# An RWKV attention and a gated feed-forward layer: the sign word made by GpSimd, and a new written order

## The chip, the cores and the metric

The kernel runs on one core of one Trainium2 chip. The metric is the device time of one execution in microseconds (us), the median of three runs. A core has five engines that each work through their own queue in order: TensorE (PE, with the loads of its stationary operand shown as PEld), VectorE (DVE), ScalarE (ACT), GpSimd (POOL) and the sync engine (SP), which here issues all the DMAs.

## The reference

```python
def _attn_ref(r, k, v, w, u):            # B 4, H 8, S 768, D 48
    state = np.zeros((B, H, D, D)); y = np.zeros_like(r)
    for t in range(S):
        kt, vt, rt = (k[:, :, t], v[:, :, t], r[:, :, t])
        cur = np.einsum('bhd,bhe->bhde', u[None] * kt, vt)
        y[:, :, t] = np.einsum('bhd,bhde->bhe', rt, state + cur)
        state = w[None, :, :, None] * state + np.einsum('bhd,bhe->bhde', kt, vt)
    return y

def _moe_ref(x, w_gate, w_val, w_out):   # 3072 tokens, d_model 384, d_ff 1536
    gate = 1.0 / (1.0 + np.exp(-(x @ w_gate)))
    return gate * (x @ w_val) @ w_out
```

The output of the attention, as 3072 rows of 384, is the input `x` of the second function. The three weight matrices come to the chip as 64-bit floating-point numbers, and the kernel turns them into 32-bit numbers itself.

## The kernel before

The attention is done in 12 chunks of 64 tokens, each in two groups of heads, so there are 24 groups `n`. For a group: `L` and `X` load its channels (512 KB) and tokens (400 KB); `A`, `R`, `k`, `T` scale keys and queries by powers of `w`; `Z` makes the scores on PE; `K` masks them on VectorE; `I` applies them and the state on PE; `O` makes the state's increment on PE; `d` (ScalarE) and `s` (VectorE) bring the state on; `h` (ScalarE) and `l` (VectorE) write the output as a rounded part and a rest into the tile `xt`; `F` moves the 16 channels left over into their places with small DMAs.

Two chunks of all batches make a tile of 512 tokens, and there are six. Each tile goes through 12 weight blocks `f`: `U` is 18 matmuls of 512 columns into two PSUM banks of a ring of three, `g` a sigmoid on ScalarE, `m` a product on VectorE, `H` the rounded part of it on ScalarE, `q` its rest on GpSimd (`qv`: on VectorE), and `D` nine matmuls into three accumulators. Block 0 of the first tile is done in two halves of 256 columns, so that `U.0`, `U.1` are the halves, `U.2` is block 1 and `U.8` block 7.

A weight block is made ready once, while the first tile is worked on. `W` loads it (1152 KB for 128 x 1152 numbers of 64 bits; block 0 in two halves). `c` on ScalarE scales the high 32-bit word, read as a float, by 2^-112 into `wf`. `j` (`join_words`) on VectorE makes the 32-bit number: shift by three, put the sign of the high word in, put the three top bits of the low word in. `w` on ScalarE rounds it into the first half of `wx`, and `o` on GpSimd (`ov`: on VectorE) writes the rest into the second half. `wx` lies in the place of the raw words `wr`.

The order of the first 13 items, from the first load to the start of the second tile, is written out as a list of steps, `START`; behind the dot stands the group, the block or the item. Each engine gets its instructions in this order. Behind the list a loop runs over the remaining items of the other five tiles with its own fixed order.

A step that waits holds back every later step of its engine: this goes for SP's queue of DMAs as for the others.

Of the kernel before, what the change touches and what calls it, by code (L numbers as in the profile page):

```python
# [39 lines left out]


START = """
tc L.0 L.1 X.0 X.1 W.0 tk L.2 X.2 A.0 ti.1 Rv.0 A.1 k.0 ti.0 Z.0 Rv.1 k.1 tp L.3 c0.1 c0.0 K.0 tt
tn T.0 j0.1 I.0 T.1 Z.1 h.0 A.2 R.2 O.0 l.0 w0.1 K.1 T.2 F.0 X.3 W.1 o0.1 W.2 s.0 W.3 L.4 j0.0 I.1
O.1 h.1 k.2 X.4 s.1 w0.0 Z.2 l.1 A.3 o0.0 L.5 K.2 c.1 F.1 U.0 k.3 Rv.3 c.2 Tv.3 Z.3 j.1 g.0 I.2
m.0 w.1 K.3 O.2 R.4 H.0 X.5 h.2 qv.0 W.4 ov.1 d.2 W.5 L.6 l.2 c.3 s.2 F.2 j.2 I.3 A.4 O.3 R.5 h.3
X.6 d.3 W.6 l.3 W.7 W.8 w.2 s.3 F.3 j.3 U.1 A.5 D.0 g.1 U.2 m.1 w.3 ov.2 H.1 ov.3 c.4 qv.1 c.5 k.4
Tv.4 Z.4 g.2 k.5 Tv.5 D.1 L.7 m.2 K.4 H.2 U.3 q.2 j.4 Z.5 g.3 m.3 w.4 I.4 K.5 H.3 O.4 h.4 R.6 ov.4
D.2 X.7 d.4 W.9 W.10 q.3 W.11 A.6 l.4 s.4 F.4 c.6 j.5 I.5 O.5 h.5 R.7 d.5 A.7 l.5 s.5 F.5 w.5 k.6
U.4 Tv.6 j.6 Z.6 g.4 ov.5 w.6 D.3 m.4 c.7 o.6 K.6 H.4 U.5 j.7 c.8 g.5 qv.4 w.7 j.8 I.6 O.6 h.6 D.4  # L50
d.6 m.5 w.8 l.6 s.6 F.6 H.5 ov.7 U.6 qv.5 c.9 ov.8 k.7 c.10 Tv.7 j.9 Z.7 g.6 D.5 m.6 U.7 w.9 K.7
H.6 o.9 j.10 g.7 q.6 c.11 I.7 O.7 h.7 D.6 d.7 m.7 l.7 H.7 s.7 F.7 w.10 q.7 j.11 U.8 ov.10 D.7 w.11
g.8 ov.11 U.9 m.8 H.8 q.8 D.8 g.9 m.9 H.9 L.8 X.8 U.10 q.9 D.9 g.10 m.10 H.10 U.11 q.10 A.8 R.8
k.8 T.8 D.10 g.11 m.11 H.11 U.12 q.11 D.11 g.12 m.12 H.12 qv.12
"""


# [1 line left out]
def rwkv_then_moe(ctx: ExitStack, tc: tile.TileContext, wd, ch, tk, wt, rk0, vn0, wd0, out):  # L59
    nc = tc.nc  # L60
# [151 lines left out]
    def scale_words(f, c):  # L212
        if f not in w32:
            w32[f] = wtmp.tile([P, W3], F32, name="wf")
        words = raw[f].bitcast(F32).rearrange("q (n two) -> q n two", two=2)
        nc.scalar.activation(w32[f][:, c], words[:, c, 1], AF.Copy, scale=2.0**-112)  # L216

    def join_words(f, c):
        words = raw[f].bitcast(I32).rearrange("q (n two) -> q n two", two=2)
        low, high = words[:, c, 0], words[:, c, 1]  # L220
        g = w32[f].bitcast(I32)[:, c]
        nc.vector.tensor_scalar(g, g, 3, None, ALU.logical_shift_left)
        nc.vector.scalar_tensor_tensor(g, high, -(2**31), g, ALU.bitwise_and, ALU.bitwise_or)
        nc.vector.scalar_tensor_tensor(g, low, 29, g, ALU.logical_shift_right, ALU.bitwise_or)

    def round_weights(f, c):
        if f not in wparts:
            wparts[f] = wp.tile([P, 2, W3], F32R, name="wx", tag=f"w{f}")
            whi[f], wlo[f] = wparts[f][:, 0], wparts[f][:, 1]
        nc.scalar.copy(out=whi[f][:, c], in_=w32[f][:, c])  # L230
# [256 lines left out]
    def accumulators():  # L487
        return [pacc.tile([P, 512], F32, name=f"acc{d}") for d in range(3)]
# [298 lines left out]
```

## Time and profile before

| | |
|---|---|
| median of three runs | 580.67 us (579.79 to 582.91) |
| the profiled execution | 580.07 us, its span 578.3 us |
| PE busy | 534.4 us, 92% of the span |
| VectorE, ScalarE, GpSimd busy | 211.7, 189.4 and 146.1 us |
| mean granted TensorE clock | 0.972 |

The profiled execution lies 0.6 us under the median and inside the runs' spread; 1.8 us of it are outside the span. PE is busy nearly all of the time from about 110 us on, so the head of the program, in which the written order rules, is where PE is idle.

### The profile page before, as it was taken

Reading aid. Unit: us, or ns where it says so; the run is one execution under the profiler, and the core shown is the slowest. Engines: PE = TensorE matmul, PEld = TensorE weight load, DVE = VectorE, ACT = ScalarE, POOL = GpSimd, SP = SyncE. Lnnn points to the kernel's source line nnn. Section 1 sums busy time; section 2 is a strip of 40 time slices with the busy share of each in tenths; the row PEclk is TensorE's granted clock in tenths of the full one; section 3 lists DMA queues with packets and bytes.
Section 4 is the critical chain, followed back from the end, with each engine's and each line's share of the span. In section 5 each row is a group of like instructions: output and inputs, shape, how many; then the busy total and the mean of one; then the engine's idle time right before and its main releaser. Section 6 shows DMA issues by size and latency. Waiting matters only on the chain. (4 is left out here: it accounts for less than half of the span.)

```text
span 578.3 us, 12857 instructions
## 1 busy us (share of the span) xinstructions
PE 534.4 (92%) x5689; PEld 431.4 (75%) x5689; DVE 211.7 (37%) x338; ACT 189.4 (33%) x420; POOL 146.1 (25%) x125
## 2 busy tenths in 40 slices
PE   3646987999999999999999999999999999999994
PEld 2635766788778878788888788888788788888883
DVE  7896899931422322412312313313313312200101
ACT  4365465432422322322322323323413212212211
POOL 3420320323232222222322313313312211221220
PEclk9766999999999999999999999999999999999998
DMA  8498340130410113320113220013130001100001
GB/s 313 160 396 329 134 203 10 22 128 0 141 48 1 29 48 84 104 83 1 35 41 84 79 109 1 13 63 85 59 128 2 9 2 19 56 0 1 1 0 60
DMA packets 13261, 44.54 MB, mean 77 GB/s; under 512 B 2096, under 2 KB 2736, under 8 KB 11792
## 3 DMA queue, kind: packets, MB, share of 16 engines
q1 hardware_dynamic: 13200, 43.66, 21.8%
q8 instruction: 46, 0.75, 0.5%
q14 instruction: 15, 0.12, 0.1%
HBM read 36.58 MB, written 4.72 MB: 71 GB/s over the span
## 5 line engine op out<-in xcount | busy, mean ns | idle before, releaser
L443 PE MATMUL ring<-xt,wx 128*128 128x512 f32 (+1 forms) x1314 | 319.8, 396 | 14.2 <-DMA xt<-xt 7.6
L443 PEld LDWEIGHTS ring<-xt,wx 128*128 128x128 f32 x1314 | 245.4, 191 | 72.6 <-issue 9.7
L465 POOL TENSOR_TENSOR h<-sg,h 128x512 fp32r<-128x512 f32 x68 | 89.6, 1317 | 362.3 <-ACT h L461 362.3
L481 PE MATMUL acc<-h,wx 128*128 128x512 f32 (+1 forms) x657 | 163.7, 394 | 0.4 <-POOLq L613 0.4
L456 DVE TENSOR_TENSOR sg<-ring,sg 128x512 f32<-128x512 f32 (+1 forms) x73 | 49.9, 684 | 289.4 <-PE ring L443 289.4
L481 PEld LDWEIGHTS acc<-h,wx 128*128 128x128 f32 x657 | 121.2, 189 | 27.6 <-POOLq L613 0.8
L461 ACT CAST h<-sg 128x512 fp32r<-128x512 f32 (+1 forms) x73 | 44.8, 614 | 148.8 <-DVE sg L456 148.8
L452 ACT ACTIVATE sg<-ring 128x512 f32<-128x512 f32 (+1 forms) x73 | 43.2, 591 | 143.3 <-PE ring L443 143.2
L323 DVE COPY_PREDICATED score<-masks,sc 128x512 f32<-128x512 int32 x48 | 36.1, 753 | 14.8 <-PE sc L315 14.0
L265 POOL TENSOR_TENSOR dec<-chan,tabk 128x512 f32<-128x512 f32 x21 | 28.2, 1342 | 20.2 <-DVE wx L233 12.8
L259 ACT ACTIVATE dec<-chan,wu 128x128 f32<-128x128 f32 x96 | 30.7, 399 | 3.0 <-DMA chan<-in_ch 3.0
L402 ACT CAST xt<-ring 112x256 fp32r<-112x256 f32 (+1 forms) x52 | 17.1, 375 | 39.8 <-PE ring L284 39.8
L406 DVE TENSOR_TENSOR xt<-ring,xt 112x256 fp32r<-112x256 f32 (+1 forms) x52 | 19.9, 418 | 26.6 <-ACT xt L402 25.2
L315 PE MATMUL sc<-dec,chan 48*64 48x64 f32 x768 | 17.2, 231 | 9.8 <-DVE chan L271 7.3
L284 PEld LDWEIGHTS ring<-dec,state 48*48 48x48 f32 (+1 forms) x704 | 13.3, 130 | 14.0 <-issue 8.7
L369 ACT ACTIVATE state<-state,pw 112x96 f32<-112x96 f32 x80 | 23.5, 366 | 0.0
L315 PEld LDWEIGHTS sc<-dec,chan 48*64 48x64 f32 x768 | 14.8, 145 | 11.6 <-DVE chan L271 7.3
L284 PEld LDWEIGHTS ring<-score,toks 64*48 64x48 f32 (+1 forms) x768 | 14.5, 136 | 10.9 <-issue 6.6
L284 PE MATMUL ring<-dec,state 48*48 48x64 f32 (+1 forms) x704 | 16.7, 227 | 6.4 <-ACT sg L452 4.6
L284 PE MATMUL ring<-score,toks 64*48 64x64 f32 (+1 forms) x768 | 18.0, 234 | 3.8 <-DVE score L323 2.4
L216 ACT ACTIVATE wf<-wr 128x1152 f32<-128x1152 f32 (+1 forms) x13 | 15.3, 1189 | 15.7 <-DMA wr<-in_wt 10.1
L275 POOL TENSOR_TENSOR toks<-toks,tabn 128x384 f32<-128x384 f32 x17 | 18.0, 1059 | 8.8 <-ACT tabn L181 8.8
(52 smaller groups left out, 211.1 us busy)
## 6 DMA issues: line engine op xcount, KB each, us to landing
wr<-in_wt SPq DMA_DIRECT2D x11, 1152.0 KB, 9.0
chan<-in_ch SPq DMA_DIRECT2D x24, 512.0 KB, 4.9
toks<-in_tk SPq DMA_DIRECT2D x24, 400.0 KB, 5.1
out_y<-wf SPq DMA_DIRECT2D x17, 256.0 KB, 2.3
xt<-xt SPq DMA_DIRECT2D x30, 64.0 KB, 2.3
wr<-in_wt SPq DMA_DIRECT2D x2, 576.0 KB, 7.2
xt<-xt SPq DMA_DIRECT2D x12, 32.0 KB, 4.9
out_y<-sg SPq DMA_DIRECT2D x2, 128.0 KB, 3.2
```

What stands on the lines that cost most here:

```text
L259: nc.scalar.activation(t[:, 1, cs], k[:, cs], AF.Copy, scale=wu[:, 1, 4 * g + m : 4 * g + m + 1])
L265: eng.tensor_tensor(v4(t[:, 0]), v4(chan[n][:, 0]), bc2(table_of(n)[:, :, ::-1]), ALU.mult)
L284: nc.tensor.matmul(yb[n][bank][64 * half : 64 * half + m, cs], lhsT, rhs, start=first, stop=stop, skip_group_check=True,)
L315: nc.tensor.matmul(sc[64 * gm : 64 * gm + 64, be, o : o + C], kk[row, cs : cs + C], rr[row, cs : cs + C], start=True, stop=True,)
L323: nc.vector.copy_predicated(t.rearrange("q (b m i) -> q b m i", b=2, m=4), masks[:, m].bitcast(I32).unsqueeze(1).unsqueeze(1).broadcast_to ...
L369: nc.scalar.activation(st[:, p, s], st[:, p, s], AF.Copy, scale=pw[0:112, 4 * g + 2 * p + s, 64:65],)
L443: nc.tensor.matmul(o[:, self.cols], w[a][:, g * DM + kt * P : g * DM + (kt + 1) * P], self.x[:, kt, b, self.cols], start=(k == 0), stop=(k ...
L452: nc.scalar.activation(sg[:, c], self.pair[f][0][:, c], AF.Sigmoid)
L456: nc.vector.tensor_tensor(sg[:, c], self.pair.pop(f)[1][:, c], sg[:, c], ALU.mult)
L461: nc.scalar.copy(out=h[:, 0, c], in_=sg[:, c])
L465: eng.tensor_tensor(h[:, 1, c], self.sg.pop(f)[:, c], h[:, 0, c], ALU.subtract)
L481: nc.tensor.matmul(self.acc[d][:, self.cols], w[a][:, 2 * DM + d * P : 2 * DM + (d + 1) * P], h[:, b, self.cols], start=(f == 0 and k == 0 ...
```

## The change

The middle one of the three VectorE passes of `join_words` falls away. A new step `z` on GpSimd reads the high words as floats, compares them with zero, multiplies the 0 or 1 by -2^31 and writes the result as an integer over the high words. That is the sign bit, or zero. VectorE then shifts and joins this sign in one pass, and joins the low word in a second. `z` of a block must come behind `c` of the block, which reads the high words, and ahead of its `j`.

The list `START` is written anew. It holds a `z` for each block, and a new step `N` of nine matmuls of the identity with itself (128 x 128), whose result nobody reads. Of the steps that can run on either engine, `o` and `T` stand more often on GpSimd: ahead of `U.8` the list had `ov` seven times and has it five times, `Tv` five times and now twice, `qv` four times and now twice. The loads stand in another order, and `l.3` now stands ahead of `O.3`.

```diff
-tc L.0 L.1 X.0 X.1 W.0 tk L.2 X.2 A.0 ti.1 Rv.0 A.1 k.0 ti.0 Z.0 Rv.1 k.1 tp L.3 c0.1 c0.0 K.0 tt
...
+L.1 tk W.0 L.0 tc ti.0 A.1 tp tt R.1 c0.1 ti.1 k.1 X.0 X.1 N.9 Rv.0 W.1 z0.1 A.0 tn L.2 X.2 c0.0
...
+    def sign_words(f, c):
+        high = raw[f].bitcast(F32).rearrange("q (n two) -> q n two", two=2)[:, c, 1]
+        out = raw[f].bitcast(I32).rearrange("q (n two) -> q n two", two=2)[:, c, 1]
+        nc.gpsimd.tensor_scalar(out, high, 0.0, -(2.0**31), ALU.is_lt, ALU.mult)
+
     def join_words(f, c):
         words = raw[f].bitcast(I32).rearrange("q (n two) -> q n two", two=2)
-        low, high = words[:, c, 0], words[:, c, 1]
+        low, sign = words[:, c, 0], words[:, c, 1]
         g = w32[f].bitcast(I32)[:, c]
-        nc.vector.tensor_scalar(g, g, 3, None, ALU.logical_shift_left)
-        nc.vector.scalar_tensor_tensor(g, high, -(2**31), g, ALU.bitwise_and, ALU.bitwise_or)
+        nc.vector.scalar_tensor_tensor(g, g, 3, sign, ALU.logical_shift_left, ALU.bitwise_or)
         nc.vector.scalar_tensor_tensor(g, low, 29, g, ALU.logical_shift_right, ALU.bitwise_or)
...
+    def idle_matmuls(k):
+        t = pacc.tile([P, 512], F32, name="acc2")
+        for _ in range(k):
+            nc.tensor.matmul(t[:, 0:P], ident, ident, start=True, stop=True)
...
+        "N": idle_matmuls,
+        "z": lambda f: sign_words(f, ALL), "z0": lambda j: sign_words(0, HALVES[j]),
```

The queue of SP at the start, before (`chan` is filled by `L`, `toks` by `X`, `wr` by `W`, and `xt<-xt` are the small DMAs of `F.0`):

```order
L101 DMA chan<-in_ch 128x1024 x2
L106 DMA toks<-in_tk 128x800 x2
L210 DMA wr<-in_wt 128x576 x2
L101 DMA chan<-in_ch 128x1024
L106 DMA toks<-in_tk 128x800
L101 DMA chan<-in_ch 128x1024
L410 DMA xt<-xt 16x2x256 x6
L106 DMA toks<-in_tk 128x800
L210 DMA wr<-in_wt 128x1152 x3
```

And after:

```order
L102 DMA chan<-in_ch 128x1024
L211 DMA wr<-in_wt 128x576 x2
L102 DMA chan<-in_ch 128x1024
L107 DMA toks<-in_tk 128x800 x2
L211 DMA wr<-in_wt 128x1152
L102 DMA chan<-in_ch 128x1024
L107 DMA toks<-in_tk 128x800
L211 DMA wr<-in_wt 128x1152
L102 DMA chan<-in_ch 128x1024
L107 DMA toks<-in_tk 128x800
L211 DMA wr<-in_wt 128x1152
L416 DMA xt<-xt 16x2x256 x6
```

Block 0 is now loaded between the two first groups' channels, and three more blocks (1, 2 and 7) stand ahead of the small DMAs, where none stood before.

GpSimd from the rest of block 0 to the rest of the next block that it makes (`wx`), before (`dec` are the queries of `R`, `h` the rests of `q`):

```order
L233 TENSOR_TENSOR wx<-wf,wx 128x576 x2
L265 TENSOR_TENSOR dec<-chan,tabk 128x512 x2
L465 TENSOR_TENSOR h<-sg,h 128x512
L265 TENSOR_TENSOR dec<-chan,tabk 128x512
L465 TENSOR_TENSOR h<-sg,h 128x512
L265 TENSOR_TENSOR dec<-chan,tabk 128x512
L233 TENSOR_TENSOR wx<-wf,wx 128x1152 x2
```

And after, with the passes of `z` (`wr<-wr`) and a `T` (`toks`):

```order
L239 TENSOR_TENSOR wx<-wf,wx 128x576 x2
L271 TENSOR_TENSOR dec<-chan,tabk 128x512
L223 TENSOR_SCALAR wr<-wr 128x1152
L271 TENSOR_TENSOR dec<-chan,tabk 128x512
L223 TENSOR_SCALAR wr<-wr 128x1152
L281 TENSOR_TENSOR toks<-toks,tabn 128x384
L239 TENSOR_TENSOR wx<-wf,wx 128x1152
L471 TENSOR_TENSOR h<-sg,h 128x256
```

`z` of blocks 1 and 2 and the rest of block 1 (`o.1`) have come between, and GpSimd has more to do in the same stretch.

VectorE at the join of block 2 and the state of group 3, before:

```order
L222 TENSOR_SCALAR wf<-wf 128x1152
L223 SCALAR_TENSOR_TENSOR wf<-wr,wf 128x1152
L224 SCALAR_TENSOR_TENSOR wf<-wr,wf 128x1152
L406 TENSOR_TENSOR xt<-ring,xt 48x2x128 x4
L379 TENSOR_TENSOR state<-state,ring 112x2x96 x2
```

And after:

```order
L229 SCALAR_TENSOR_TENSOR wf<-wf,wr 128x1152
L230 SCALAR_TENSOR_TENSOR wf<-wr,wf 128x1152
L277 TENSOR_TENSOR chan<-chan,tabk 128x512
L412 TENSOR_TENSOR xt<-ring,xt 48x2x128 x4
L385 TENSOR_TENSOR state<-state,ring 112x2x96 x2
```

The join has two passes instead of three, and the keys of group 4 (`k.4`, `chan`) now stand between it and `l.3`, behind which `O.3` on PE now waits.

More of the change, by code (lines that the diff above doesn't have):

```diff
@@ L42 @@
 START = """
-tc L.0 L.1 X.0 X.1 W.0 tk L.2 X.2 A.0 ti.1 Rv.0 A.1 k.0 ti.0 Z.0 Rv.1 k.1 tp L.3 c0.1 c0.0 K.0 tt
[L44 to L54, printed above, removed]
+L.1 tk W.0 L.0 tc ti.0 A.1 tp tt R.1 c0.1 ti.1 k.1 X.0 X.1 N.9 Rv.0 W.1 z0.1 A.0 tn L.2 X.2 c0.0
+k.0 Z.0 j0.1 z0.0 K.0 T.0 T.2 c.1 I.0 h.0 T.1 O.0 j0.0 Z.1 W.2 L.3 s.0 w0.1 l.0 X.3 K.1 W.7 w0.0
+I.1 o0.1 A.2 O.1 Rv.2 h.1 F.0 o0.0 A.3 k.2 s.1 Z.2 l.1 R.3 U.0 K.2 c.2 k.3 L.4 g.0 I.2 h.2 O.2 z.1
+R.4 d.2 X.4 z.2 Z.3 A.4 j.1 W.5 m.0 L.5 W.3 T.3 H.0 l.2 K.3 s.2 j.2 I.3 w.1 o.1 h.3 k.4 W.11 q.0
+R.5 d.3 c.3 l.3 W.4 O.3 F.2 s.3 Z.4 w.2 W.6 U.1 z.3 Tv.4 A.5 g.1 ov.2 L.7 k.5 m.1 H.1 D.0 q.1 j.3
+K.4 U.2 c.4 g.2 m.2 w.3 D.1 U.3 H.2 L.6 z.4 ov.3 j.4 g.3 X.5 Z.5 I.4 O.4 W.8 c.5 K.5 m.3 W.10 q.2
+z.5 R.6 h.4 D.2 l.4 d.4 s.4 H.3 j.5 A.6 I.5 d.5 h.5 T.5 O.5 k.6 w.5 o.5 A.7 s.5 X.6 F.1 l.5 qv.3
+w.4 Z.6 U.4 g.4 Rv.7 c.7 D.3 ov.4 k.7 K.6 z.7 c.6 U.5 g.5 m.4 z.6 Z.7 H.4 I.6 d.6 Tv.6 O.6 j.7 j.6
+h.6 w.6 X.7 m.5 s.6 H.5 l.6 q.4 F.6 ov.6 D.4 K.7 c.8 U.6 q.5 w.7 g.6 W.9 ov.7 z.8 D.5 c.9 m.6 H.6
+j.8 q.6 U.7 g.7 I.7 T.7 F.5 O.7 D.6 F.4 z.9 w.8 d.7 o.8 h.7 m.7 H.7 s.7 l.7 c.10 qv.7 j.9 U.8 g.8
+z.10 D.7 m.8 w.9 H.8 o.9 c.11 qv.8 F.3 j.10 U.9 g.9 F.7 D.8 L.8 X.8 U.10 z.11 m.9 w.10 j.11 H.9
+g.10 qv.9 m.10 H.10 w.11 qv.10 A.8 R.8 k.8 T.8 o.10 D.9 U.11 ov.11 g.11 m.11 D.10 H.11 U.12 qv.11
+g.12 m.12 H.12 qv.12 D.11
 """
```

## The prediction

> **What bounds the kernel now.** I read the strips of the page first, then four windows, then PE in order of time, then the forms on VectorE and GpSimd. The strip shows PE at its limit from the eighth slice on, with gaps only ahead of it.
>
> ```profile
> PE   3646987999999999999999999999999999999994
> ...
> GB/s 313 160 396 329 134 203 10 22 128 0 141 48 1 29 48 84 104 83 1 35 41 84 79 109 1 13 63 85 59 128 2 9 2 19 56 0 1 1 0 60
> ```
>
> In the windows the columns are the length, then the busy time of PE, PEld, VectorE, ScalarE and GpSimd with their instructions, the granted clock, the DMA share and GB/s.
>
> ```profile
> 0.00:13.00 13.00, 3.21 (x73) 2.68 (x76) 9.64 (x22) 5.54 (x13) 3.63 (x15) 1.00 0.83 311
> 13.00:49.00 36.00, 17.66 (x530) 16.20 (x531) 31.08 (x48) 19.10 (x46) 11.27 (x8) 0.69 0.73 278
> 49.00:111.20 62.20, 56.03 (x830) 45.25 (x830) 55.82 (x66) 33.68 (x61) 13.36 (x7) 0.96 0.35 134
> 111.20:578.30 467.10, 457.50 (x4262) 367.28 (x4262) 115.17 (x204) 131.11 (x302) 117.87 (x95) 0.99 0.15 47
> ```
>
> Behind 111.2 us PE works 457.50 of 467.10 us: nothing in the change touches that work, and a start of `U.8` that comes earlier by some us ends the kernel earlier by as much. Ahead of it VectorE is the fullest engine: 86.9 of the 98.2 us between 13 and 111.2, and 55.82 of 62.20 in the later part, where PE has only 6.17 us to lose. GpSimd works 24.6 us in the two windows. PE in order of time gives the four places on which I build (start, duration, idle time ahead with its releaser):
>
> ```profile
> 8.23 1.08 PE L315 MATMUL sc<-chan,dec 48*64 48x64 f32 x32
> 11.37 1.09 PE L176 MATMUL acc<-ident,sg 128*128 128x128 f32 x4 [2.06 <-DVE sg L170]
> ...
> 49.00 4.18 PE L443 MATMUL ring<-xt,wx 128*128 128x256 f32 x18 [7.64 <-DMA xt<-xt]
> ...
> 111.17 4.44 PE L443 MATMUL ring<-xt,wx 128*128 128x512 f32 x18 [0.99 <-DVE sg L456]
> ```
>
> The first scores end at 9.31, `U.1` starts at 49.00 behind a wait of 7.64 us for the small DMAs of `F.2`, and `U.8` starts at 111.17.
>
> **What VectorE loses.** The forms (count, then busy us and mean ns):
>
> ```profile
> L223 DVE SCALAR_TENSOR_TENSOR wf<-wr,wf 128x1152 int32<-128x1152 int32 x11 | 17.0, 1548 | 0.4
> ...
> L224 DVE SCALAR_TENSOR_TENSOR wf<-wr,wf 128x1152 int32<-128x1152 int32 x11 | 15.9, 1444 | 0.4
> L233 DVE TENSOR_TENSOR wx<-wf,wx 128x1152 fp32r<-128x1152 f32 x9 | 12.4, 1385 | 0.0
> ...
> L222 DVE TENSOR_SCALAR wf<-wf 128x1152 int32<-128x1152 int32 x11 | 11.8, 1072 | 2.3 <-ACT wf L216 2.3
> ...
> L275 DVE TENSOR_TENSOR toks<-toks,tabn 128x384 f32<-128x384 f32 x5 | 2.8, 553 | 0.0
> ...
> L465 DVE TENSOR_TENSOR h<-sg,h 128x512 fp32r<-128x512 f32 x3 | 2.1, 688 | 0.7 <-ACT h L461 0.7
> ...
> L222 DVE TENSOR_SCALAR wf<-wf 128x576 int32<-128x576 int32 x2 | 1.3, 640 | 0.0
> ...
> L465 DVE TENSOR_TENSOR h<-sg,h 128x256 fp32r<-128x256 f32 x2 | 0.8, 414 | 0.0
> ```
>
> The pass that falls away is the cheap one, and its mean of 1072 ns is not its own price. Six rows of the two engines in order of time show what is in it:
>
> ```profile
> 12.66 0.44 DVE L222 TENSOR_SCALAR wf<-wf 128x576 int32<-128x576 int32 x1
> ...
> 70.81 0.75 DVE L222 TENSOR_SCALAR wf<-wf 128x1152 int32<-128x1152 int32 x1
> ...
> 104.10 2.67 DVE L222 TENSOR_SCALAR wf<-wf 128x1152 int32<-128x1152 int32 x1
> 106.80 2.32 DVE L223 SCALAR_TENSOR_TENSOR wf<-wr,wf 128x1152 int32<-128x1152 int32 x1
> 109.16 1.36 DVE L224 SCALAR_TENSOR_TENSOR wf<-wr,wf 128x1152 int32<-128x1152 int32 x1
> ...
> 103.47 2.68 POOL L233 TENSOR_TENSOR wx<-wf,wx 128x1152 fp32r<-128x1152 f32 x1 [18.25 <-ACT wx L230]
> 106.11 1.80 POOL L465 TENSOR_TENSOR h<-sg,h 128x512 fp32r<-128x512 f32 x1
> ```
>
> Alone it takes 0.75 us. At 104.10 GpSimd was in the middle of a pass that ended at 106.15, and VectorE's ended 0.62 us behind that; the next pass, 2.32 us instead of 1.36, ended 1.2 us behind GpSimd's second. So these passes do not run beside GpSimd's: one waits for the other. The blocked time in the quoted forms is 11 x (1.072 - 0.75) + 2 x (0.640 - 0.44) + 11 x (1.548 - 1.36) + 11 x (1.444 - 1.36) = 6.9 us, or 0.28 of GpSimd's 24.6 us.
>
> Ahead of `U.8` the new order has ten blocks joined (0 to 9). The pass saved is 9 x 0.75 + 2 x 0.44 = 7.6 us. Two `ov` fewer save 2 x 1.35 = 2.7 (at nearly their mean), three `Tv` fewer 3 x 0.55 = 1.7, and of the four `qv` two half-width ones go, 0.8. Together 12.8 us. That the old order also joined block 10 ahead of `U.8`, and the new one does not, I count at nothing: PE waited only 0.99 us there. The two joins left are of L223's form, and I leave their price.
>
> **What GpSimd gets, and what that costs VectorE.** No row shows `z`. The nearest GpSimd rows:
>
> ```profile
> L465 POOL TENSOR_TENSOR h<-sg,h 128x512 fp32r<-128x512 f32 x68 | 89.6, 1317 | 362.3 <-ACT h L461 362.3
> ...
> L275 POOL TENSOR_TENSOR toks<-toks,tabn 128x384 f32<-128x384 f32 x17 | 18.0, 1059 | 8.8 <-ACT tabn L181 8.8
> L233 POOL TENSOR_TENSOR wx<-wf,wx 128x1152 fp32r<-128x1152 f32 x2 | 5.4, 2688 | 27.9 <-ACT wx L230 27.9
> ...
> L126 POOL COPY masks<-causal 64x64 f32<-64x64 f32 x2 | 0.5, 232 | 0.1
> ...
> L121 POOL TENSOR_SCALAR_AFFINE_SELECT causal<-causal 128x128 f32<-128x128 f32 x1 | 0.3, 292 | 0.1
> ```
>
> From the two rows with one input, 60 ns for 64 more elements, 1152 elements cost 0.23 + 1088 x 0.94 ns = 1.25 us; with two inputs the same size takes 2.69. I take 1.5, near the rows with one input, a fifth more for two operations and every second word. Ten blocks give 15.0. The `T` that moved add 3 x 1.06 = 3.2, one more `o` 2.7, one `q` and two half-width ones 1.3 + 1.5 = 2.8. GpSimd gets 23.7 us more, on 24.6. It has room for that (48 of 98 us), but each of its us may block VectorE: 0.28 of it by what I measured, 0.65 if it falls on VectorE blindly, since the quoted forms fill 64.1 of 98.2 us. I take 0.40, nearer the measured share, but higher, because GpSimd's passes now queue behind each other: 9.5 us. VectorE's net relief is 3.3 us.
>
> In GpSimd's queue `z` waits for its `c`, which waits for the load; `R`, `T` and `q` stand behind it, and `Z`, `O` and `D` on PE wait for those. The loads come early enough (below) that I add nothing; the bound is one such wait of a load, 4.86 us.
>
> For one-input passes the Trainium skill, in GPSIMD Engine Reference, Engine selection, says that they run at roughly line rate; with its clock of 1.2 GHz that is an estimate of 0.96 us for `z`, by which the time would be 571.7 instead of 573.9. No run here shows it yet.
>
> **The order.** VectorE's own waits, the load that stood behind one, and the DMAs by size:
>
> ```profile
> 11.25 1.51 DVE L323 COPY_PREDICATED score<-masks,sc 128x512 f32<-128x512 int32 x2
> ...
> 29.98 0.76 DVE L222 TENSOR_SCALAR wf<-wf 128x1152 int32<-128x1152 int32 x1 [2.35 <-ACT wf L216]
> ...
> 53.29 0.42 DVE L456 TENSOR_TENSOR sg<-ring,sg 128x256 f32<-128x256 f32 x1 [4.83 <-PE ring L443]
> ...
> 28.72 1.23 ACT L216 ACTIVATE wf<-wr 128x1152 f32<-128x1152 f32 x1 [4.86 <-DMA wr<-in_wt]
> ...
> wr<-in_wt SPq DMA_DIRECT2D x11, 1152.0 KB, 9.0
> chan<-in_ch SPq DMA_DIRECT2D x24, 512.0 KB, 4.9
> toks<-in_tk SPq DMA_DIRECT2D x24, 400.0 KB, 5.1
> ```
>
> Blocks 1 and 2 are now loaded ahead of the small DMAs, so the 2.35 us go. Block 0 ahead of `L.0` puts 1152 KB in its way, at 311 GB/s 3.8 us: the first scores end at 13.1 instead of 9.31, later than the 11.25 at which VectorE was ready to mask them, which costs 1.9. Ahead of the fills of `F.2` stand eight blocks, six `L` and five `X`, 14.6 MB, at the 396 GB/s of the third slice 37 us: they land near 42, not 49. But PE must first do `O.3`, now behind `l.3`, which stands behind a join and `k.4` on VectorE, both open to GpSimd's passes; so I count half of VectorE's 4.83 us, 2.4. The nine idle matmuls, 9/4 x 1.09 = 2.5 us, lie behind the transposes and ahead of scores that wait for `L.0`: nothing, and if that cover were gone 2.5.
>
> The sum: 3.3 + 2.35 + 2.4 - 1.9 = 6.15 us, so 580.07 becomes 573.9. The median of 580.67 is 0.6 higher, inside the spread of the three runs.
>
> **The rivals.** (1) The exclusion eats the gain: at 0.65 the 23.7 us cost 15.4, and 12.8 - 15.4 + 2.85 = +0.25 gives 579.8. For it speaks that VectorE blocked at 104.10 stood in front of PE's wait at 111.17. A rule that speaks for it: the Trainium skill, Perfetto Trace Analysis, Optimizing Scalar/DVE Operations, warns that VectorE and GpSimd share a read port, so that moving work between them might not help; the rows at 104 to 109 agree. (2) Slower: `z` is as dear as a pass with two inputs. Then 26.9 + 8.7 = 35.6 us are added, at 0.65 that is 23.1, and 12.8 - 23.1 + 2.85 = -7.5 gives 587.5. It decides from the point where added time x share passes 15.65. (3) Faster: the blocked times fall where VectorE would wait anyhow, and PE's own work is the limit: 7.64 + 6.17 of PE's idle time go, less the 1.9, so 568.2. (4) GpSimd becomes the bound: its work ahead of `U.8` is 33.3 us and ten `z`, and it reaches 111 at 7.8 us for each `z`; every us above adds 10. No GpSimd row comes near, so its chance is small. The Trainium skill, GPSIMD Engine Reference, Elementwise — side-by-side cycle accounting, gives some 12 cycles an element where code branches on data; that would make 11.5 us and, as an estimate, 617; a comparison need not branch, and no run here shows it.
>
> **How the numbers follow.** My case 0.42 (571 to 577), even 0.21 (577 to 583), faster 0.20 (565 to 571), slower 0.13, GpSimd as the bound 0.04. About 0.5%, 2.9 us, can be told from no change here, so faster ends at 577.2: 0.62, 0.21, 0.17. The range is 566 to 585: it leaves out the last two cases for the most part and the far end of the faster one.
>
> **What would show it.** Right: thirteen rows of `z` near 1.5 us; VectorE's joins with two rows a block, some of 2 to 3 us beside a GpSimd row; `U.1` at 44 to 48; `U.8` near 105; the rest as before. Wrong: `z` far from 1.5, `U.1` still at 49, or new PE waits for VectorE between `U.4` and `U.8`.

## The result, and the profile after

The changed kernel takes 599.6 us (median of 4 runs, 597.5 to 605.5) against 580.23 us (579.02 to 582.91) for the kernel before on the same chip: ratio 1.0356, interval 1.0309 to 1.0402. The forecast was 573.9 us with a range of 566 to 585; the time lies far above it. The profiled execution took 597.5 us, with a span of 595.7 us at a mean granted clock of 0.956.

The strips of PE and GpSimd on the page after (a digit is the busy tenth of 14.9 us):

```profile
PE   3649797994999999999999989999999999999994
...
POOL 7787765785033133223222312322312211121220
```

Before, PE was at its limit from the eighth slice on. Now there is a gap in the tenth slice (134 to 149 us), and GpSimd, which had 24.6 us of work between 13 and 111 us, is busy for most of the slices up to there. The windows after, with the stretch behind 111.2 us cut once more at 150 (columns as before: length, then PE, PEld, VectorE, ScalarE, GpSimd, clock, DMA share, GB/s):

```profile
13.00:49.00 36.00, 19.03 (x618) 16.88 (x610) 28.04 (x41) 18.92 (x45) 29.27 (x15) 0.71 0.95 351
49.00:111.20 62.20, 54.60 (x694) 44.91 (x692) 57.78 (x51) 28.43 (x51) 39.92 (x15) 0.87 0.25 89
111.20:150.00 38.80, 29.68 (x190) 23.21 (x179) 28.02 (x20) 13.17 (x23) 27.82 (x9) 0.87 0.18 55
150.00:595.70 445.70, 434.25 (x4163) 348.45 (x4161) 105.18 (x192) 123.15 (x288) 108.69 (x88) 1.00 0.14 45
```

Between 111.2 and 150 us PE works 29.68 of 38.80 us, at a clock of 0.87. GpSimd has 27.82 us of work there. The forms on GpSimd and on VectorE (count, busy us, mean ns, idle time ahead):

```profile
L223 POOL TENSOR_SCALAR wr<-wr 128x1152 int32<-128x1152 f32 x11 | 50.4, 4590 | 7.6 <-ACT wf L217 7.6
L239 POOL TENSOR_TENSOR wx<-wf,wx 128x1152 fp32r<-128x1152 f32 x5 | 15.6, 3121 | 5.1 <-ACT wx L236 5.1
L223 POOL TENSOR_SCALAR wr<-wr 128x576 int32<-128x576 f32 x2 | 4.6, 2308 | 2.5 <-ACT wf L217 2.5
...
L229 DVE SCALAR_TENSOR_TENSOR wf<-wf,wr 128x1152 int32<-128x1152 int32 x11 | 26.4, 2399 | 3.7 <-POOL wr L223 3.6
L230 DVE SCALAR_TENSOR_TENSOR wf<-wr,wf 128x1152 int32<-128x1152 int32 x11 | 22.9, 2082 | 0.4
L239 DVE TENSOR_TENSOR wx<-wf,wx 128x1152 fp32r<-128x1152 f32 x6 | 12.1, 2022 | 1.0 <-ACT wx L236 1.0
```

`z` takes 4.59 us in the mean and 4.24 where nothing is in its way, not the 1.5 us of the sum. VectorE's joins take 2.40 and 2.08 us where 1.36 is the price of such a pass alone. VectorE lost one pass of a block and is busy 229.3 us, 17.6 more than before. PE in order of time shows where the time went:

```profile
45.51 0.42 PE L290 MATMUL ring<-toks 64*64 64x48 f32 x2 [6.30 <-DVE xt L412]
...
49.06 3.71 PE L449 MATMUL ring<-xt,wx 128*128 128x256 f32 x18
...
114.83 4.34 PE L449 MATMUL ring<-xt,wx 128*128 128x512 f32 x18
...
142.43 1.65 PE L487 MATMUL acc<-h,wx 128*128 128x512 f32 x3 [8.28 <-DVE h L471]
143.88 6.05 PE L449 MATMUL ring<-xt,wx 128*128 128x512 f32 x18
```

`U.1` starts at 49.06, as before: it no longer waits 7.64 us for the small DMAs, but `O.3` ahead of it waits 6.30 us for `l.3` on VectorE, which stands behind the join of block 2 and `k.4`. `U.8` starts at 114.83, 3.7 us later than before. `U.11` starts at 143.88, where it started at 130.05 before: another 10.2 us, behind a wait of 8.28 us in `D.9` for the rest that VectorE writes in `qv.9`. By `U.13` the lag is 15.5 us, and the spans differ by 17.4.

Two places of the trace after show how a dear `z` gets in the way. The first is the join of blocks 7 and 6:

```profile
82.47 8.48 POOL L223 TENSOR_SCALAR wr<-wr 128x1152 int32<-128x1152 f32 x2 [3.96 <-ACT wf L217]
...
83.48 3.31 DVE L281 TENSOR_TENSOR toks<-toks,tabn 128x384 f32<-128x384 f32 x1
86.77 5.04 DVE L229 SCALAR_TENSOR_TENSOR wf<-wf,wr 128x1152 int32<-128x1152 int32 x1
```

`z.7` ends at 86.7. At that moment the join of block 7 on VectorE is released, and at the same moment GpSimd begins `z.6`. VectorE's pass starts at 86.77 and ends at 91.81, 0.9 us behind `z.6`: 5.04 us instead of 1.36. The pass ahead of it, 0.55 us alone, had been held to 3.31 by `z.7`.

The second is a ring of three engines behind `U.8`. `wf` has two buffers, so ScalarE's `c` of a block waits for the `o` two blocks earlier, and that `o` stands in GpSimd's queue with the `z`:

```profile
115.95 2.77 POOL L239 TENSOR_TENSOR wx<-wf,wx 128x1152 fp32r<-128x1152 f32 x1
118.75 1.28 ACT L217 ACTIVATE wf<-wr 128x1152 f32<-128x1152 f32 x1 [4.80 <-POOL wx L239]
120.12 5.31 POOL L223 TENSOR_SCALAR wr<-wr 128x1152 int32<-128x1152 f32 x1 [1.40 <-ACT wf L217]
125.39 2.74 POOL L239 TENSOR_TENSOR wx<-wf,wx 128x1152 fp32r<-128x1152 f32 x1
128.16 1.29 ACT L217 ACTIVATE wf<-wr 128x1152 f32<-128x1152 f32 x1 [5.12 <-POOL wx L239]
129.53 5.32 POOL L223 TENSOR_SCALAR wr<-wr 128x1152 int32<-128x1152 f32 x1 [1.41 <-ACT wf L217]
...
134.89 2.40 DVE L229 SCALAR_TENSOR_TENSOR wf<-wf,wr 128x1152 int32<-128x1152 int32 x1 [3.56 <-POOL wr L223]
137.33 2.03 DVE L230 SCALAR_TENSOR_TENSOR wf<-wr,wf 128x1152 int32<-128x1152 int32 x1
139.29 3.09 DVE L471 TENSOR_TENSOR h<-sg,h 128x512 fp32r<-128x512 f32 x1
```

From `z.10` at 120.12 to `z.11` at 129.53 are 9.41 us: `z` 5.3, `o` 2.7, and 1.4 in which GpSimd waits for `c`. PE takes a block every 6.26 us where nothing holds it (two neighbouring `U` in the run with a small `z`, below). Then `j.11` waits for `z.11`, `qv.9` stands behind `j.11` in VectorE's queue, and `D.9` on PE waits for `qv.9`: the 8.28 us.

### The profile page after: what moved, and what is told of

Same layout as the page of the kernel before. It is cut to its first block, busy times and chain, and to the rows that moved or that the text cites. A ratio compares the mean times of both kernels' runs of the same rounds, so it can differ in the third digit from the quotient of the medians.

```text
span 595.7 us, 12894 instructions
## 1 busy us (share of the span) xinstructions
PE 542.3 (91%) x5707; PEld 438.1 (74%) x5707; DVE 229.3 (38%) x321; ACT 189.4 (32%) x420; POOL 214.3 (36%) x142
## 5 line engine op out<-in xcount | busy, mean ns | idle before, releaser
L449 PE MATMUL ring<-xt,wx 128*128 128x512 f32 (+1 forms) x1314 | 325.0, 401 | 9.6 <-DVE sg L462 3.5
L449 PEld LDWEIGHTS ring<-xt,wx 128*128 128x128 f32 x1314 | 249.8, 195 | 69.1 <-issue 4.6
L471 POOL TENSOR_TENSOR h<-sg,h 128x512 fp32r<-128x512 f32 (+1 forms) x66 | 89.7, 1360 | 347.4 <-ACT h L467 347.4
L223 POOL TENSOR_SCALAR wr<-wr 128x1152 int32<-128x1152 f32 (+1 forms) x13 | 55.1, 4239 | 10.1 <-ACT wf L217 10.1
L229 DVE SCALAR_TENSOR_TENSOR wf<-wf,wr 128x1152 int32<-128x1152 int32 (+1 forms) x13 | 27.9, 2145 | 3.7 <-POOL wr L223 3.6
L230 DVE SCALAR_TENSOR_TENSOR wf<-wr,wf 128x1152 int32<-128x1152 int32 (+1 forms) x13 | 24.8, 1908 | 0.4
L290 PE MATMUL ring<-toks 64*48 64x48 f32 (+1 forms) x704 | 16.3, 222 | 8.4 <-DVE xt L412 6.7
L290 PEld LDWEIGHTS ring<-score,toks 64*48 64x48 f32 (+1 forms) x768 | 13.9, 132 | 11.8 <-issue 6.5
L290 PE MATMUL ring<-score,toks 64*64 64x64 f32 (+1 forms) x768 | 17.4, 229 | 4.9 <-DVE score L329 2.0
L281 POOL TENSOR_TENSOR toks<-toks,tabn 128x384 f32<-128x384 f32 x20 | 21.1, 1057 | 1.5 <-DMA toks<-in_tk 1.5
```

The lines of the kernel that those rows point to most:

```text
L223: nc.gpsimd.tensor_scalar(out, high, 0.0, -(2.0**31), ALU.is_lt, ALU.mult)
L229: nc.vector.scalar_tensor_tensor(g, g, 3, sign, ALU.logical_shift_left, ALU.bitwise_or)
L290: nc.tensor.matmul(yb[n][bank][64 * half : 64 * half + m, cs], lhsT, rhs, start=first, stop=stop, skip_group_check=True,)
L449: nc.tensor.matmul(o[:, self.cols], w[a][:, g * DM + kt * P : g * DM + (kt + 1) * P], self.x[:, kt, b, self.cols], start=(k == 0), stop=(k ...
L471: eng.tensor_tensor(h[:, 1, c], self.sg.pop(f)[:, c], h[:, 0, c], ALU.subtract)
```

## The experiments

Each time is the median in us; the ratio, formed from the single runs and not from the two medians, is to the kernel before on the same chip in the same rounds (its medians were 579.1 to 580.2).

### Is it the order or the sign pass?

`old_order_z` keeps the order of before, without the idle matmuls, and puts each `z` right behind its `c`:

```diff
-L.1 tk W.0 L.0 tc ti.0 A.1 tp tt R.1 c0.1 ti.1 k.1 X.0 X.1 N.9 Rv.0 W.1 z0.1 A.0 tn L.2 X.2 c0.0
+tc L.0 L.1 X.0 X.1 W.0 tk L.2 X.2 A.0 ti.1 Rv.0 A.1 k.0 ti.0 Z.0 Rv.1 k.1 tp L.3 c0.1 z0.1 c0.0 z0.0 K.0 tt
...
```

> The order of before, with the sign pass on GpSimd put right behind each scaling pass, and the two-pass join; nothing else. Theory A (price: the GpSimd pass takes 4.24 us instead of 1.5, and for all of it VectorE's passes with two SBUF inputs stand still): GpSimd gets 55 us in the head and VectorE saves 9.2 us; at a blocked share of 0.4 to 0.65 that is 13 to 27 us of loss, so 593 to 607 us. Theory B (the written order itself is worse, the pass is harmless): about 575 us, faster than before by some of the 9 us saved.

Measured: 608.07, ratio 1.0504 (1.0465 to 1.0544).

`new_order_old_join` has the new order without its `z`, and the join of before in three passes:

```diff
...
-        nc.vector.scalar_tensor_tensor(g, g, 3, sign, ALU.logical_shift_left, ALU.bitwise_or)
+        nc.vector.tensor_scalar(g, g, 3, None, ALU.logical_shift_left)
+        nc.vector.scalar_tensor_tensor(g, high, -(2**31), g, ALU.bitwise_and, ALU.bitwise_or)
```

> The new order with all sign passes left out and the three-pass join of before on VectorE. Theory A: the loss goes; the new order is worth its other terms, 572 to 580 us. Theory B: the loss stays, 592 us or more, since VectorE even gets a pass more.

Measured: 582.37, ratio 1.0038 (1.0012 to 1.0063).

`new_thin_sign` is the changed kernel with `z` on the first 64 columns of each block:

```diff
     def sign_words(f, c):
+        c = slice(c.start, c.start + 64)
```

> The changed kernel, with each sign pass done on 64 of its columns only (the signs of the other columns are left out, so that their weights are not those of the reference): all instructions and waits stay, the pass is nearly free. Theory A: the rows of the sign pass fall from 4.2 to about 0.4 us, and the time falls below before, 566 to 575 us. Theory B: no change from the changed kernel, 597 us.

Measured: 573.79, ratio 0.9914 (0.9884 to 0.9943). Its forms, and PE in order of time:

```profile
L224 POOL TENSOR_SCALAR wr<-wr 128x64 int32<-128x64 f32 x13 | 8.8, 680 | 13.4 <-ACT wf L217 13.4
...
L231 DVE SCALAR_TENSOR_TENSOR wf<-wr,wf 128x1152 int32<-128x1152 int32 x11 | 21.0, 1908 | 0.4
L230 DVE SCALAR_TENSOR_TENSOR wf<-wf,wr 128x1152 int32<-128x1152 int32 x11 | 16.8, 1524 | 0.0
```

```profile
102.59 4.34 PE L450 MATMUL ring<-xt,wx 128*128 128x512 f32 x18
...
121.36 4.33 PE L450 MATMUL ring<-xt,wx 128*128 128x512 f32 x18
127.62 4.36 PE L450 MATMUL ring<-xt,wx 128*128 128x512 f32 x18
```

With the same steps, waits and order, a `z` of 0.68 us gives the forecast time, and `U.8` starts at 102.59. So the size of `z` makes the loss. The order alone is no gain, and the new order stands the dear `z` better than the old one, by 8.5 us.

### The price of the sign pass by itself

`prices` is the kernel before with nine GpSimd passes behind the end, when VectorE is idle (`fs`, `js` are every second word of a tile as float and integer, `fc`, `jc` 576 neighbouring words, `pt` all 1152):

```diff
+    nc.gpsimd.tensor_scalar(js, fs, 0.0, -(2.0**31), ALU.is_lt, ALU.mult)
+    nc.gpsimd.tensor_scalar(jc, fc, 0.0, -(2.0**31), ALU.is_lt, ALU.mult)
...
+    nc.gpsimd.tensor_scalar(fs, fs, 0.0, 2.0, ALU.min, ALU.mult)
+    nc.gpsimd.tensor_scalar(fc, fc, 0.0, None, ALU.is_lt)
...
+    nc.gpsimd.tensor_copy(fc, fc)
+    nc.gpsimd.tensor_scalar(pt, pt, 2.0, None, ALU.mult)
```

> The kernel of before with nine one-input GpSimd passes added behind its end, on a tile that nobody else uses, to price the pass when VectorE stands idle (576 elements a partition, the last one 1152). If the pass is dear in itself, the first one takes 2.1 us or so as the half-width rows of the changed kernel (2.3), if it is dear only beside VectorE, about 0.7. If the comparison is the dear part, the passes with is_lt take 2.1 and those with mult or min alone 0.7; if the change of type is, those that write integers are the dear ones; if every second word is, the first and fourth are.

The rows of GpSimd in that order:

```profile
574.41 2.19 POOL L615 TENSOR_SCALAR wf<-wf 128x576 int32<-128x576 f32 x1
576.68 2.13 POOL L616 TENSOR_SCALAR wf<-wf 128x576 int32<-128x576 f32 x1
...
581.12 2.19 POOL L618 TENSOR_SCALAR wf<-wf 128x576 f32<-128x576 f32 x1
583.38 1.66 POOL L619 TENSOR_SCALAR wf<-wf 128x576 f32<-128x576 f32 x1
...
588.58 0.67 POOL L622 COPY wf<-wf 128x576 f32<-128x576 f32 x1
589.33 3.12 POOL L623 TENSOR_SCALAR wf<-wf 128x1152 f32<-128x1152 f32 x1
```

A tensor-scalar pass costs 2.7 ns an element with one operation (3.12 us for 1152) and 3.7 with two; a copy costs 1.2. Comparison or minimum, integer or float, every second word or neighbours: all within 3%. So `z` is dear in itself, not because VectorE is in its way. The Trainium skill, GPSIMD Engine Reference, Engine selection, calls passes with one input roughly line rate; the copy comes near that, the tensor-scalar pass does not, and the measurement decides.

### How the time grows with the price

`half_sign` and `three_quarters_sign` put `z` on half and on three quarters of the columns:

```diff
+        c = slice(c.start, (c.start + c.stop) // 2)
...
+        c = slice(c.start, c.start + 3 * (c.stop - c.start) // 4)
```

> After, with the sign pass on the first half of each block's columns alone (the signs of the other half are left out). By the prices, z on 576 elements takes 2.1 to 2.3 us instead of 4.24, so GpSimd has 11 x 2.1 = 23 us less than after and about 19 us more than with 64 columns. If the loss goes with the price of z, in a straight line from 573.8 us (z of 0.68) to 599.6 (z of 4.24), this run gives 584 to 586. If GpSimd's chain behind U.8 bounds only from a threshold on, the run lies below the line, 575 to 580. If what costs is that the joins wait for z at all, however short it is behind its c, it lies above the line, 590 or more.

> After, with the sign pass on three quarters of each block's columns (the last quarter's signs left out), so z of about 3.2 to 3.5 us. With 64 columns (0.68 us) the time was 573.8, with half 577.8 (z mean 2.50), with all 599.6 (4.58). A straight line between the last two gives 587 to 590. If the loss is a queue on GpSimd that overflows only near the full price, it lies well below, 580 to 584. If the blocked passes on VectorE alone make it, it follows VectorE's excess, which grew by 0.3 us a block from 64 columns to half and by 1.1 from half to all, and comes out near 586.

Measured: 577.83, ratio 0.9968 (0.9943 to 0.9993), and 584.82, ratio 1.0085 (1.0062 to 1.0108). The rows of their `z`, one of each run:

```profile
L224 POOL TENSOR_SCALAR wr<-wr 128x576 int32<-128x576 f32 x11 | 27.4, 2499 | 6.9 <-ACT wf L217 6.9
```

```profile
L224 POOL TENSOR_SCALAR wr<-wr 128x864 int32<-128x864 f32 x11 | 39.8, 3620 | 9.6 <-ACT wf L217 9.6
```

| mean of `z` in us | 0.68 | 2.50 | 3.62 | 4.59 |
|---|---|---|---|---|
| time | 573.8 | 577.8 | 584.8 | 599.6 |
| VectorE busy | 204.6 | 211.4 | 213.4 | 229.3 |

The curve bends: each us of `z` costs 2.2, then 6.2, then 15.2 us of time. It is neither a straight line nor a sharp edge, as two of the theories had it; and the third, that the blocked passes alone make the loss, does not fit from half to three quarters, where the time grows by 7.0 us and VectorE's busy time by 2.0. The last slope is above the 12 that would come if every `z` (eleven and two halves) stood on the path with its full length, so something besides its length is added there. The last row of the table shows it: from three quarters to all columns VectorE's busy time grows by 15.9 us.

### Time on GpSimd, reads, and the wait of the join

First with the join in three passes, where nobody needs `z`. `idle_sign` is `new_order_old_join` with the same operations of `z` on an idle tile of 1088 numbers of 16 bits, `idle_memset` with seven fills (four for half blocks) in their place, which read nothing:

```diff
+        nc.gpsimd.tensor_scalar(scratch[:, n], scratch[:, n], 0.0, -(2.0**31), ALU.is_lt, ALU.mult)
...
+        for _ in range(7 if c == ALL else 4):
+            nc.gpsimd.memset(s, 1.0)
```

> The new order with the three-pass join (582.4 us by itself), and in the place of each sign pass a GpSimd pass with the same two operations on 1088 numbers of a tile that nobody else uses: nobody waits for its result. Its price should be near 4.0 us. Theory A1 (GpSimd's reading shuts VectorE's two-input passes out while the pass runs): the loss comes back without any dependence, 598 to 612 us. Theory A2 (VectorE loses time because its join waits for the result of the sign pass): 582 to 585 us.

> As the run with the idle sign pass, but in its place seven fills of 544 numbers (four for a half block), which read nothing, 3.9 us in all. GpSimd is as busy, and what stands behind in its queue is as late. Theory A1: VectorE's passes with two inputs run beside it, 582 to 588 us. Theory A3 (what hurts is that the queries, token keys and rests behind the pass in GpSimd's queue come late): as the run with the idle sign pass, 595 us or more.

Measured: 588.74, ratio 1.0152 (1.0126 to 1.0177), and 586.42, ratio 1.0105 (1.0085 to 1.0125), against 582.37 without them. GpSimd's time alone makes 4.0 us, the reads of this stand-in 2.3 more. That the reads of `z` itself do no more is not shown by it, since the stand-in turns out to be unlike `z` in that point (below).

Then in the changed kernel itself. `free_join` and `free_join_fills` keep its order and its join in two passes and make the same two replacements; the join takes the high words as they are:

> After, with its order and its joins of two passes, but the full-priced sign pass (two operations, 4.25 us) works on an idle tile of 1088 bf16 and nobody waits for it; the joins take the unchanged high words, so the signs are left out. Against 64 columns (573.8) this adds only GpSimd's time and its reads, against after (599.6) it lacks only the wait of the join for z and of z for c. If GpSimd's lateness and the blocked passes make the loss, 594 to 600. If the wait of the joins makes the convex part of it, 580 to 586.

> The same with seven fills of 544 elements (four for half blocks) in place of each pass, which read nothing and take the same time. If reading is what costs VectorE, this is 2 to 6 us below free_join (it was 2.3 us below in the pair with joins of three passes); if only GpSimd's time counts, the same.

Measured: 581.76, ratio 1.0045 (1.0007 to 1.0083), and 581.03, ratio 1.0012 (0.9963 to 1.0061). So of the 25.8 us between a small and a full `z`, about 7 come with GpSimd's time alone and 1 or less with the reads of the stand-in; 17.8 come only with the real `z`. By its design `free_join` lacks the wait of the join for `z` and of `z` for `c`. Its rows show that it lacks something more. The forms:

```profile
L225 POOL TENSOR_SCALAR scratch<-scratch 128x1088 bf16<-128x1088 bf16 x11 | 48.0, 4367 | 0.1
...
L232 DVE SCALAR_TENSOR_TENSOR wf<-wr,wf 128x1152 int32<-128x1152 int32 x11 | 23.5, 2137 | 0.4
L231 DVE SCALAR_TENSOR_TENSOR wf<-wf,wr 128x1152 int32<-128x1152 int32 x11 | 15.2, 1386 | 0.0
```

GpSimd is as busy as after (213.0 and 214.3 us), but VectorE is busy 213.7 us, where it has 229.3 after: 15.6 us less. The first pass of the join takes 1.39 us here and 2.40 after. One VectorE pass shows why. `ov.7` writes the rest of block 7. It does not wait for the GpSimd pass of block 8, and in three runs it starts about a microsecond behind that pass's start. After, beside `z` on all 1152 columns:

```profile
101.30 4.25 POOL L223 TENSOR_SCALAR wr<-wr 128x1152 int32<-128x1152 f32 x1 [0.27 <-ACT wf L217]
102.29 4.12 DVE L239 TENSOR_TENSOR wx<-wf,wx 128x1152 fp32r<-128x1152 f32 x1 [0.95 <-ACT wx L236]
```

In `three_quarters_sign`, beside `z` on 864 columns:

```profile
93.97 3.23 POOL L224 TENSOR_SCALAR wr<-wr 128x864 int32<-128x864 f32 x1 [0.23 <-ACT wf L217]
94.97 1.36 DVE L240 TENSOR_TENSOR wx<-wf,wx 128x1152 fp32r<-128x1152 f32 x1 [0.92 <-ACT wx L237]
```

In `free_join`, beside the stand-in:

```profile
93.21 3.88 POOL L225 TENSOR_SCALAR scratch<-scratch 128x1088 bf16<-128x1088 bf16 x1
94.47 1.36 DVE L241 TENSOR_TENSOR wx<-wf,wx 128x1152 fp32r<-128x1152 f32 x1 [0.93 <-ACT wx L238]
```

Only the full-width `z` holds the pass, until about half a microsecond before its own end; beside the other two the pass runs at its price, inside the GpSimd pass. Added up over the rows, with each VectorE pass set against the shortest of its form, `z` holds VectorE for about 19 us after, for 2 in `three_quarters_sign`, and the stand-in for 3 in `free_join`; this is an estimate. `three_quarters_sign` has all the waits of the changed kernel, if for a `z` that is 1 us shorter, and its VectorE is as little busy (213.4 us) as that of `free_join`, where nobody waits for the pass. So the growth of VectorE's busy time comes with the hold and not with the wait. How the 17.8 us of time divide between the hold and the wait is not shown: no run has a full-width `z` on 32-bit numbers that nobody waits for. The Trainium skill, SBUF — State Buffer, Who interferes with whom, says that a VectorE instruction with two SBUF inputs contends with a GpSimd instruction that reads SBUF; the 5.04 us at 86.77 and the 4.12 us at 102.29 agree, the two passes of 1.36 us do not.

### Relief in single places

`late_join` moves one join of the changed kernel, `j.11`, behind `qv.9`:

```diff
-z.10 D.7 ... z.11 m.9 w.10 j.11 H.9 g.10 qv.9 m.10
+z.10 D.7 ... z.11 m.9 w.10 H.9 g.10 qv.9 j.11 m.10
```

> The changed kernel with the join of block 11 moved behind the rest of item 9 on VectorE, and nothing else. If the wait of 8.3 us that PE has for that rest in the changed kernel comes from the join that waits for the last sign pass, it goes, and with it the slow clock behind it: 588 to 592 us. If the rest is late for other reasons: 597 us or more.

Measured: 601.23, ratio 1.0384 (1.0336 to 1.0432). The wait of `D.9` is gone, and PE waits in `U.11` instead. In its waits (in all, times, longest):

```profile
PE ring L449 <- POOL wx L239: 6.5, 2, 5.9
```

`rest_on_vector` puts `o.8`, `o.9`, `o.10` on VectorE:

```diff
-... w.8 d.7 o.8 h.7 ... H.8 o.9 c.11 ... T.8 o.10 D.9
+... w.8 d.7 ov.8 h.7 ... H.8 ov.9 c.11 ... T.8 ov.10 D.9
```

> After, with the full sign pass, but the rest-of-weights passes of blocks 8, 9 and 10 on VectorE (1.35 us each alone) instead of GpSimd (3.12 us each). 9.4 us leave GpSimd in the stretch where it is the fuller engine, 4 to 6 us come to VectorE. If GpSimd's queue is what bounds PE there, 585 to 593. If VectorE's time and its blocked passes bound, 600 to 606. The nearest earlier run, one join moved, changed nothing (601.2).

Measured: 599.69, ratio 1.0361 (1.0328 to 1.0394). GpSimd's work between 111.2 and 150 us falls from 27.8 to 20.0 us, and VectorE's rises from 28.0 to 30.9. The ring stays closed, through VectorE:

```profile
112.93 9.64 POOL L223 TENSOR_SCALAR wr<-wr 128x1152 int32<-128x1152 f32 x2
...
118.40 5.02 DVE L229 SCALAR_TENSOR_TENSOR wf<-wf,wr 128x1152 int32<-128x1152 int32 x1
...
127.49 1.28 ACT L217 ACTIVATE wf<-wr 128x1152 f32<-128x1152 f32 x1 [0.91 <-DVE wx L239]
```

`c.11` starts at 127.49 here and at 128.16 after. The join of block 9 at 118.40 is held by `z.10`. So neither GpSimd's queue nor one late join is the bound alone; as I read the rows, the two `wf` buffers tie `c`, `z`, `j` and `o` together. A third buffer wasn't tried.

`sign_early_only` has `z` for blocks 0 to 7 only, and joins 8 to 11 in three passes:

```diff
+        if f < 8:
             nc.vector.scalar_tensor_tensor(g, g, 3, sign, ALU.logical_shift_left, ALU.bitwise_or)
+        else:
+            nc.vector.tensor_scalar(g, g, 3, None, ALU.logical_shift_left)
+            nc.vector.scalar_tensor_tensor(g, sign, -(2**31), g, ALU.bitwise_and, ALU.bitwise_or)
```

> After, but blocks 8 to 11 are joined in three passes on VectorE as before; only blocks 0 to 7 have z. Of the loss of 15.5 us by U.13, 3.7 us were there at U.8, 11.8 arose behind it. If z, GpSimd's queue and the joins that wait for it make that part, it goes: 583 to 588. The four z taken away are 17 us of GpSimd; the four passes given back are 3 to 4.3 us of VectorE. If the order is what starves PE there, whoever makes the sign, 595 or more.

Measured: 588.6, ratio 1.0166 (1.0142 to 1.0191): 11.0 us come back, although VectorE has four passes more. Between `U.8` (112.08) and `U.13` (147.69) 4.2 us of the 11.8 are left. Most of the loss behind `U.8` is therefore due to the last four `z`, not to the order.

### The sign on ScalarE, and the idle matmuls

`act_sign` makes the sign word on ScalarE, with a factor of 0, which, other than I expected, leaves the signs out; `act_tiny` with 2^-140, which does keep them, so that nothing of the computation is left out; `act_tiny_old` is `act_tiny` with the order of before:

```diff
...
-        nc.gpsimd.tensor_scalar(out, high, 0.0, -(2.0**31), ALU.is_lt, ALU.mult)
+        nc.scalar.activation(high, high, AF.Copy, scale=2.0**-140)
```

> The changed kernel with the sign word made by ScalarE, at the same places of the order: the high word as a float times 0.0, written as a float, is plus or minus zero, which is the sign bit alone. ScalarE gets thirteen passes of about 1.2 us, GpSimd none. Theory A: the loss goes, as with the thin sign pass (573.8), unless ScalarE's own steps get late: 571 to 578 us. Theory B: no better than the new order with the three-pass join, 582 us.

> After, with the sign made by ScalarE: the high word as a float times 2^-140, which leaves a zero or a tiny number of the same sign; whether the sign survives so small a number is not known, and no other part of the computation is touched. If the price of GpSimd's pass is the failed term, this is as fast as the ScalarE pass with factor 0, 574 to 580 (578.25 there). If the loss comes from a third pass over the block that the join waits for, 590 or more.

> The same ScalarE sign with the order of before and the sign pass right behind each block's scaling. VectorE loses the 7.6 us of the third pass; the order's gains are absent. If the order is worth the 2.85 us that I gave it and ScalarE's 13 passes of about 1.2 us hide beside its third of busy time, 575 to 580 (3 us above the new order). If the old order with z (608) was slow for its order rather than for GpSimd's price, 585 or more.

Measured: 578.25, ratio 0.9953 (0.9929 to 0.9977); 578.17, ratio 0.9954 (0.9937 to 0.9972); 578.67, ratio 0.9964 (0.9942 to 0.9987). The pass on ScalarE:

```profile
L222 ACT ACTIVATE wr<-wr 128x1152 f32<-128x1152 f32 x11 | 14.0, 1277 | 0.1
```

The third pass of a block off VectorE is no loss where its engine does it in 1.28 us, although the join waits for it all the same. The gain is small: 0.4 to 0.5%.

`thin_no_idle` and `act_tiny_no_idle` take the nine idle matmuls out of `new_thin_sign` and `act_tiny`:

```diff
-L.1 tk W.0 ... X.0 X.1 N.9 Rv.0 W.1
+L.1 tk W.0 ... X.0 X.1 Rv.0 W.1
```

> After, with the sign pass on 64 columns (other signs left out) and without the nine idle matmuls. If they are hidden, as the prediction has it, 573 to 575, the same as with them (573.8). If they keep the granted clock up for the work behind them, 576 to 580.

> The new order with ScalarE's sign pass (578.2) and without the nine idle matmuls. With 64 columns on GpSimd taking them out was worth 2.1 us (573.8 to 571.7). If they stand in PE's way ahead of scores that are ready, 575.5 to 577; if that difference was chance, 578.

Measured: 571.7, ratio 0.9835 (0.9814 to 0.9856), and 576.8, ratio 0.9959 (0.9942 to 0.9976). The first pair differs by 2.1 us in the medians, with intervals that do not meet; the second by 1.4, with nearly equal ratios (0.9954 and 0.9959). The profiled spans of the first pair are 570.0 and 570.1 us, and `U.8` starts at 102.59 and 102.21. Whether the matmuls cost something is not settled; no run shows a use of them. Of the versions here that do everything, `act_tiny` and `act_tiny_no_idle` are the fastest, 0.4 to 0.5% below the kernel before: no more than I had said could be told, but with intervals that stay under 1.

## Why the prediction was wrong

**The price of `z`: the term that failed.** "I take 1.5, near the rows with one input" was wrong by 2.8 times, and the upper bound of 2.69 from a pass with two inputs was too low as well. The rows that I interpolated were a copy and a select; the instruction of `z` is neither: against a copy's 1.2 ns an element it costs 2.7 with one operation and 3.7 with two. By its own formula the sum gives with 4.24 us a GpSimd load of 42.4 + 8.7 = 51.1 us, a loss of 20.4, and 12.8 - 20.4 + 2.85 = -4.8: `U.8` at 116.0. It started at 114.83. With 1.5 us the line between the first two points of the table gives 575.6, beside the 573.9 forecast.

**The stretch that the sum covered: the second failure.** "Behind 111.2 us ... nothing in the change touches that work" did not hold. Joins, `z` and `o` of the last blocks stand behind `U.8`, and 11.8 of the 15.5 us by `U.13` arose there. I had counted ten blocks and given the rest no term.

**The blocked share.** It was not one number. From a small to a full `z`, VectorE's busy time grows by 24.7 us for 48.8 us more of GpSimd (0.51); from a small one to three quarters by 8.8 for 35.5 (0.25), and with the 16-bit stand-in by 9.1 for 47.5 (0.19). My 0.40 lay between, and was near enough ahead of `U.8`. What decides is how long a pass holds VectorE, and the sum took this for a fixed part of how long it lasts.

**The order.** I had +2.85 us. With the join in three passes it is 2.7 us slower than the old order (582.4 and 579.7), with ScalarE's sign the same (578.2 and 578.7), with the full `z` 8.5 faster. `U.1` came at 49.06 after, not at 44 to 48, and at 47.73 with the small `z`. The loads did their part: `U.1` no longer waits for the small DMAs. But the wait of `O.3` for `l.3`, 6.30 us after and 5.66 with the small `z`, took the place of that wait. I had named this risk and priced it at half of 4.83 us. The sum has no term that depends on the rest in the way that the three comparisons show.

**The rivals.** Slower (2) had the right sign and the exclusion as its cause, but its price ended at 587.5. With 4.24 us and the share of 0.65 its formula, as that of (1), would give 597.6; that this is near the measured time would be luck, since it counts the stretch ahead of `U.8`, where 3.7 us arose. GpSimd as the bound (4) named an engine of the ring. I put its point at a `z` of 7.8 us, since I counted GpSimd's work up to 111 us; the ring with `c` and `o` closes far earlier, as a cycle of 9.41 us against PE's 6.26 shows. But GpSimd alone is not the bound there, as `rest_on_vector` shows. Faster (3) was wrong.

**What held.** The removed pass and the relief of VectorE: with a `z` that costs little, `U.8` starts at 102.59 ("near 105"). That the time is then 573.8, the forecast, is luck: for a `z` of 0.68 us the sum by its own formula gives 570.6, and the gain of the order in it was not there. The first scores ended at 13.34, near the 13.1 that I had worked out. By the profiled spans the idle matmuls are hidden, as forecast; by the medians that is open. The joins beside a GpSimd row did take 2 to 5 us. The signs of being wrong that I had named came too: a `z` far from 1.5, `U.1` still at 49, and PE waiting 3.48 us for VectorE at `U.6`, if at a place where it waited 1.98 us before.

**What stays open.** About 1.9 us of the spans' 17.4 arise behind `U.13`, and I have no cause for them. How the 17.8 us divide between the hold of VectorE, the wait of the join and the ring was not separated by a run. Nor was it tried where between 864 and 1152 columns the hold becomes long, or whether the number of elements or their size decides it.

## What to carry to other kernels

Price an operation on an engine by a row of the same instruction with the same number of operations; where there is none, a single pass behind the end of the kernel settles it before anything is built on it. When work moves to another engine, look for the ring that it joins: buffers that come free late, the engine that feeds it and the one that waits, and compare one turn of the ring with the consumer's pace, over all blocks and not up to a chosen point. When a pass is replaced by a stand-in to see what it costs, give the stand-in the same width and type, and look in the trace whether it does to its neighbours what the real pass does: here one of the same length, on 16-bit numbers, did not hold the other engine.

## What the runs showed of the hardware that I had not expected

- GpSimd's tensor-scalar pass costs 2.7 ns an element with one operation and 3.7 with two, against 1.2 for a copy; type, stride and a comparison change that by 3% at most.
- GpSimd's passes are lengthened too: the same `z` took 4.24 us alone and 5.3 beside VectorE's joins at 120.12 and 129.53.
- How long a GpSimd pass with one input holds VectorE's passes with two inputs is not set by its own length alone: a `z` on 1152 columns held one that came 1 us behind its start until half a microsecond before its own end (4.12 us instead of 1.36), a `z` on 864 columns and a pass on 1088 16-bit numbers of 3.88 us let one that came as late run at its price.
- Fills that read nothing cost the kernel nearly as much as a pass of the same time that reads 16-bit numbers (581.0 and 581.8 us).
- ScalarE makes the sign word of 128 x 1152 words in 1.28 us, less than a third of GpSimd's time; its product with 2^-140 keeps the sign, its product with 0 does not.
